# Pool waits by tile for the second phase of an attention, channel mix and expert kernel

## The chip, the cores and the metric

The kernel runs on one core of one Trainium2 chip. The metric is the device time of one execution in microseconds (us).

## The reference

Three parts follow each other on a batch of 4. The first is attention with 8 heads of 64 over 32 global and 512 local positions: the global queries see everything, the local ones the global keys and a band of 32 positions on either side. Its output (4 x 544 rows, 512 wide) goes through a channel mix: `r * v` with `v = relu(xk @ w_k)^2 @ w_v` and `r = sigmoid(xr @ w_r)`, where `xk` and `xr` blend each row with the one before it. The last part sends each of the 2176 rows to one of 8 experts:

```python
for s in range(S):
    fresh_e = int(np.argmax(logits[b, s]))
    if s == 0 or local_gate[b, s] < 0.5: e = fresh_e
    else: e = prev_e if prev_e >= 0 else fresh_e
    prev_e = e
    ls = logits[b, s] - logits[b, s].max()
    p = np.exp(ls)
    p /= p.sum() + 1e-09
    h = np.maximum(x[b, s] @ w1[e], 0.0)
    out[b, s] = p[e] * (h @ w2[e])
```

`w1` is 512 x 1024 and `w2` 1024 x 512 for each expert. All is float32.

## The kernel before

Each float32 product is made of three matmuls on a high and a low half (`mm3`, lines 19 to 24): an operand is copied into a tile of rounded values by ScalarE (ACT), and the rest is taken by a subtraction on VectorE (DVE) or GpSimd (POOL).

**Phase 1** (`phase1`, line 702) computes attention, channel mix and routing. The order of its work is written by a planner (`Sched`) with costs and priorities. Its tiles in SBUF lie in the pools `cf` (the mask, two `xT`, the weights `wr`) and `cs` (all else), its tiles in PSUM in two more; all four are closed at the end of phase 1. Each row is stored to `y` in DRAM. Routing leaves lists of rows by expert: `idx` (row numbers, 128 per chunk), `pcol` (gate values) and `counts` (chunks per expert). Already in phase 1, expert 0's first chunk of 128 rows is computed in gaps of TensorE (`ahead`, line 788); its output `oa` lies in `cs` and goes to `out` by an indirect DMA on GpSimd's queue (line 844).

**Phase 2** (`Experts`, lines 845 to 972) runs the eight experts. Line 996 opens its pools over the bytes that phase 1 gave back: `xwork` (two staging tiles `sw`, the gathered rows `xs1`, three pairs of transposed rows `x`), `work` (`hh`, `hl`, `hs`, `osb`), the PSUM pools `pst` (transposes, tag `pt`) and `ps2` (`ph` and `po`), and line 998 `wq` (weight slot 3). The pool `right` is older: it holds `xs0`, the staging tiles `st` and slot 2, and is in use in phase 1 already. `run` stands under a manual schedule, so that each engine keeps the written order:

```python
for k in range(K): s.gather(0,k)
_,cs=s.nc.values_load_multi_w_load_instructions(s.counts[0:1,0:E],...); cmax=...
for hf in range(2): s.prep(at(0,0),0,hf)
s.gather(1,0)
s.fetch()
for e in range(E):
    s.first(at(e,0),at(e,1),e,cs[e],...)
```

`gather` (line 857) fetches 2 x 128 rows of `y` by two indirect DMAs on GpSimd's queue, into `xs0` for the even and `xs1` for the odd chunk pairs. Line 950 loads the counts into registers of every engine. `prep` (lines 858 to 867) transposes the rows on TensorE into `pt` (line 864), ACT copies them into `xh` (line 866), DVE subtracts into `xl` (line 867). `fetch` starts weight loads of 512 KB each on SyncE's queue (line 767) into whatever staging tile is free, `st` or `sw`; `whole` (lines 776 and 779) splits a staged part into high and low on ACT and on DVE or POOL, and fetches the next.

`first` (line 933) decides by the expert's count, on every engine, with the branches of lines 937 and 941: two or more chunks take `full` (two chunks at once, lines 868 to 884) and then `more` (branches of lines 930 and 931); a single chunk takes `tail` (lines 885 to 913). In both the splits of the next expert's weights (`W`) and the transposes of its first chunks (`X`) are mixed in at fixed places. Here expert 0 has one chunk left and takes `tail`: its hidden layer goes into `pht` (line 905), its output into `po` (line 918), with expert 1's transposes after the first and fourth of eight steps of the output. `output` scales `po` into `osb` on DVE and scatters it to `out` by an indirect DMA (line 923).

The order at the seam of the two phases comes from these: the program order of each queue, the waits that a closed pool leaves to the next one on its bytes, and the branch at line 937.

## Time and profile before

| what | value |
|---|---|
| median of 3 runs | 809.23 us (805.88 to 812.53) |
| the profiled execution | 809.45 us |
| its span, first to last instruction | 807.7 us |
| busy: PE | 743.1 us (92%) |
| busy: DVE | 521.9 us (65%) |
| busy: ACT | 398.6 us (49%) |
| busy: POOL | 370.8 us (46%) |

All times in the text are us from the start of the span. PE is TensorE, PEld its weight loads, which run beside its matmuls; DVE is VectorE, ACT ScalarE, POOL GpSimd, SP SyncE. A `q` behind an engine's name means its sequencer, which waits, branches and issues DMAs. "Idle before" is the time that an engine stood still ahead of an instruction, and the releaser is what ended it, as inferred from semaphores; the one put down is the last by the profile, which is not always the one that was binding.

### The profile page before, as it was taken

What the parts mean: (1) busy time and instruction counts of PE and PEld (TensorE: products, weight loads), DVE (VectorE), ACT (ScalarE), POOL (GpSimd) and SP (SyncE); (2) the same over time, 40 slices, a digit from 0 to 9 for tenths busy, and PEclk for the clock granted to TensorE, in tenths of its full rate; (3) what the DMA queues carried; (4) which work ended last, traced back from release to release, by engine and by line L of the source; (5) the groups of instructions that cost most, each with busy time, mean ns of one, the idle gap of its engine ahead of it and who ended that gap; (6) DMA issues with size and microseconds to landing.
All of it is one profiled execution on the core that took longest, in us unless ns stands there. A gap on an engine that the chain in (4) does not pass through costs nothing. (4 is left out here: it accounts for less than half of the span.)

```text
span 807.7 us, 14233 instructions
## 1 busy us (share of the span) xinstructions
PE 743.1 (92%) x4790; PEld 626.2 (78%) x4790; DVE 521.9 (65%) x1482; ACT 398.6 (49%) x985; POOL 370.8 (46%) x495
## 2 busy tenths in 40 slices
PE   5988799899989999899999999986899999999974
PEld 3655687698878888888887888865698999998953
DVE  6699789776695785785675855664772725435531
ACT  4787676663555654655553523414661615224420
POOL 6678968645254362654462333115753513324130
PEclk9998999999999999899999899998999999999987
DMA  6674341211102102112001400317874524517210
GB/s 151 160 190 141 84 114 56 76 23 47 41 19 76 35 18 67 40 33 63 22 2 61 149 27 14 131 40 258 286 266 148 189 103 131 177 61 253 87 53 7
DMA packets 93966, 78.71 MB, mean 97 GB/s; under 512 B 70559, under 2 KB 74655, under 8 KB 93859
## 3 DMA queue, kind: packets, MB, share of 16 engines
q1 hardware_dynamic: 89618, 64.27, 26.7%
q0 software_dynamic: 4240, 13.11, 4.8%
q8 instruction: 54, 0.88, 0.5%
q14 instruction: 54, 0.43, 0.2%
HBM read 68.44 MB, written 9.70 MB: 97 GB/s over the span
## 5 line engine op out<-in xcount | busy, mean ns | idle before, releaser
L222 POOL TENSOR_SCALAR pl<-pl,mx 128x192 f32<-128x192 f32 (+1 forms) x128 | 66.9, 535 | 75.7 <-DVE mx L219 42.8
L216 ACT ACTIVATE pl<-pl,mx 128x224 f32<-128x224 f32 (+1 forms) x128 | 58.8, 461 | 35.3 <-DVE mx L213 30.4
L21 PE MATMUL psk<-xs,slot0h 128*128 128x256 f32 x256 | 75.3, 299 | 0.9 <-ACT xs L448 0.8
L23 PE MATMUL psk<-xs,slot0h 128*128 128x256 f32 x256 | 74.0, 290 | 0.0
L24 PE MATMUL psk<-xs,slot0l 128*128 128x256 f32 x256 | 73.9, 290 | 0.0
L857 POOL DMA_INDIRECT xs<-y,idx x32 | 39.9, 1246 | 70.8 <-PE pt L864 42.1
L923 POOL DMA_INDIRECT out_dram<-osb,idx x19 | 23.5, 1238 | 95.4 <-DVE osb L922 79.9
L450 POOL TENSOR_TENSOR xs<-xm,xs 128x512 fp32r<-128x512 f32 (+1 forms) x36 | 46.2, 1293 | 44.3 <-ACT xs L448 44.3
L878 ACT ACTIVATE hh<-ph 128x256 fp32r<-128x256 f32 x56 | 21.6, 385 | 84.1 <-PE ph L24 82.9
L443 POOL TENSOR_SCALAR xm<-xT,mut 128x256 f32<-128x256 f32 (+7 forms) x96 | 42.9, 465 | 29.5 <-DVE xT L294 16.2
L21 PE MATMUL psv<-slot1h,kh 128*128 128x512 f32 x136 | 55.6, 410 | 0.0
L23 PE MATMUL psv<-slot1l,kh 128*128 128x512 f32 x136 | 54.8, 404 | 0.3 <-POOL slot1l L417 0.3
L24 PE MATMUL psv<-slot1h,kl 128*128 128x512 f32 x136 | 54.7, 405 | 0.0
L21 PEld LDWEIGHTS psk<-xs,slot0h 128*128 128x128 f32 x256 | 49.4, 195 | 2.3 <-ACT xs L448 1.2
L23 PEld LDWEIGHTS psk<-xs,slot0h 128*128 128x128 f32 x256 | 49.8, 195 | 0.7
L24 PEld LDWEIGHTS psk<-xs,slot0l 128*128 128x128 f32 x256 | 49.6, 194 | 0.5
L228 PE MATMUL ptp<-ident,pl 128*128 128x128 f32 x256 | 45.1, 298 | 4.7 <-DVE qT L119 1.4
L236 PE MATMUL av<-ph,v 128*128 128x256 f32 x192 | 44.6, 292 | 2.3 <-DVE xT L294 1.0
L119 DVE TENSOR_TENSOR plo<-ptp,ph 128x512 fp32r<-128x512 f32 x48 | 32.8, 685 | 19.4 <-ACT ph L117 19.1
L879 DVE SCALAR_TENSOR_TENSOR hl<-ph,hh 128x256 fp32r<-128x256 f32 x56 | 23.7, 423 | 33.0 <-ACT hh L878 32.6
L446 DVE SCALAR_TENSOR_TENSOR xm<-xT,mut,xm 128x256 f32<-128x256 f32 (+7 forms) x96 | 40.3, 456 | 3.6 <-POOL xm L443 3.5
L228 PEld LDWEIGHTS ptp<-ident,pl 128*128 128x128 f32 x256 | 32.1, 152 | 11.5 <-POOL pl L222 3.9
(730 smaller groups left out, 2491.9 us busy)
## 6 DMA issues: line engine op xcount, KB each, us to landing
st<-in_moe_w_dram SPq DMA_DIRECT2D x42, 512.0 KB, 4.6
sw<-in_moe_w_dram SPq DMA_DIRECT2D x22, 512.0 KB, 4.8
y<-r SPq DMA_DIRECT2D x17, 256.0 KB, 2.1
qn<-in_q_l_dram SPq DMA_DIRECT2D x32, 128.0 KB, 3.0
kn<-in_k_l_dram SPq DMA_DIRECT2D x32, 128.0 KB, 3.0
earlyh<-in_moe_w_k_dram SPq DMA_DIRECT2D x8, 512.0 KB, 5.0
raw<-in_moe_w_v_dram SPq DMA_DIRECT2D x8, 512.0 KB, 4.0
vn<-in_v_l_dram SPq DMA_DIRECT2D x24, 96.0 KB, 2.1
```

The costliest lines, as they stand in the source:

```text
L21: i=nc.tensor.matmul(out,wh,xh,start=first,stop=False)
L23: nc.tensor.matmul(out,wh,xl,start=False,stop=False)
L24: return nc.tensor.matmul(out,wl,xh,start=False,stop=last)
L119: nc.vector.tensor_sub(out[1],x,out[0].bitcast(F32))
L216: nc.scalar.activation(p[:,h,ks],p[:,h,ks],AF.Exp,bias=mx[:,h:h+1],scale=-1.0,accum_out=mx[:,4+h:5+h])
L222: nc.gpsimd.tensor_scalar(out=p[:,h,ks],in0=p[:,h,ks],scalar1=mx[:,6+h:7+h],scalar2=0.0,op0=ALU.mult,op1=ALU.add)
L228: nc.tensor.transpose(pt[:,c,h],p[:,h,c*96:c*96+P],s.ident)
L236: nc.tensor.matmul(o,s.v(u,x,i,c),P_[y][:,c],start=c==m==0,stop=c==1 and m==len(parts)-1)
L443: nc.gpsimd.tensor_scalar(out=x[:,u,o:o+k],in0=s.xT[b][:,c,q:q+k],scalar1=m[:,1,c:c+1],scalar2=0.0,op0=ALU.mult,op1=ALU.add)
L446: nc.vector.scalar_tensor_tensor(out=x[:,u,o:o+k],in0=s.xT[b][:,c,1+q:1+q+k],scalar=m[:,0,c:c+1],in1=x[:,u,o:o+k],op0=ALU.mult,op1=ALU.add)
L450: nc.gpsimd.tensor_sub(xl[:,cs,:n],x[:,:,:n],xh[:,cs,:n].bitcast(F32))
L857: s.nc.gpsimd.indirect_dma_start(out=s.xs[i][:,j,:],out_offset=None,in_=s.y,in_offset=IndirectOffsetOnAxis(ap=s.idx[:,ch:ch+1],axis=0))
```

## The change

The pools that phase 2 opens are declared with `reuse_waits="tile"` in place of the default `"pool"`. With the default, the first instruction on a pool that lies on bytes given back by another waits for the users of the whole pools that lay there. With `"tile"`, the first write of each tile waits for the users of the bytes under that tile. Sizes, places, instructions and their written order are as before.

```diff
--- before.py
+++ after.py
@@ -993,9 +993,10 @@
             m=phase1(tc,st,ins,const,y,ident,x,slots,early,place,right)
             x.idx,x.pcol,x.counts,x.cmax=m.idx,m.acc[:,E*NCH:],m.ci,m.cm
 
-        x.xwork=p("xwork"); x.work=p("work"); x.ps=Pools("pt",p("pst",space=PSUM),p("ps2",space=PSUM))
+        t=dict(reuse_waits="tile")
+        x.xwork=p("xwork",**t); x.work=p("work",**t); x.ps=Pools("pt",p("pst",space=PSUM,**t),p("ps2",space=PSUM,**t))
         x.alloc()
-        slots.append(pair(p("wq"),3))
+        slots.append(pair(p("wq",**t),3))
         with tc.manual_schedule():
             x.run()
```

## Rows read from the trace of the kernel before

**Rows 1.** PE's waits, 535 to 808: us in total, times, longest.

```profile
PE pt L864 <- DMA xs<-y,idx: 4.4, 3, 2.3
PE pht L21 <- ACT xh L866: 3.4, 1, 3.4
PE pht L21 <- DMA st<-in_moe_w_dram: 2.5, 1, 2.5
```

**Rows 2.** Stretches: length; busy PE, PEld, DVE, ACT, POOL; clock, DMA share, GB/s.

```profile
543.00:550.00 7.00, 2.09 (x14) 1.50 (x13) 1.24 (x3) 0.92 (x2) 1.34 (x2) 0.76 0.23 82
550.00:558.50 8.50, 8.49 (x31) 6.42 (x31) 5.19 (x6) 5.15 (x7) 6.88 (x5) 0.79 0.83 254
558.50:562.00 3.50, 0.56 (x3) 0.40 (x4) 1.23 (x1) 1.54 (x2) 2.69 (x3) 1.00 1.04 392
568.00:574.00 6.00, 3.54 (x10) 2.80 (x10) 5.52 (x5) 3.17 (x3) 5.09 (x3) 0.72 0.88 313
574.00:776.00 202.00, 201.26 (x1256) 180.33 (x1255) 104.25 (x134) 85.08 (x135) 75.78 (x50) 1.00 0.48 162
```

**Rows 3.** Timeline of the seam: start, length, instruction [idle before <- releaser].

```profile
540.30 0.97 POOL L857 DMA_INDIRECT xs<-y,idx  x1 [19.04 <-DVE cint L699]
...
541.58 0.94 POOL L857 DMA_INDIRECT xs<-y,idx  x1 [0.30 <-issue]
...
544.55 1.03 POOL L844 DMA_INDIRECT out_dram<-oa,idx  x1 [2.03 <-DVE acc L683]
...
545.41 0.98 PE L864 MATMUL pt<-ident,xs 128*128 128x128 f32 x7 [1.46 <-DMA xs<-y,idx]
549.09 1.09 ACT L866 ACTIVATE xh<-pt 128x512 fp32r<-128x512 f32 x2 [12.22 <-DMA out_dram<-oa,idx]
549.51 1.68 SPq L767 DMA_DIRECT2D sw<-in_moe_w_dram  x2
549.69 0.98 POOL L857 DMA_INDIRECT xs<-y,idx  x1 [4.11 <-ACT xh L866]
...
549.85 0.77 PE L21 MATMUL pht<-slot2h,xh 128*128 128x512 f32 x1 [3.45 <-ACT xh L866]
```

**Rows 4.** The chain of waits, 540 to 575: start, length, what.

```profile
544.55 4.35 DMA out_dram<-oa,idx
...
553.55 8.15 DMA xs<-y,idx
```

**Rows 5.** SyncE's own waits, 535 to 575.

```profile
SPq L767 <- DMA out_dram<-oa,idx: 5.1, 1, 5.1
```

**Rows 6.** Users of `xT` and `wrh`: durations min/median/max in ns, first and last start.

```profile
L446 DVE SCALAR_TENSOR_TENSOR xm<-xT,mut,xm x96: 239/470/1251, 75.4 to 495.4; 128x256 f32<-128x256 f32 x40, 128x32 f32<-128x32 f32 x8, 128x224 f32<-128x224 f32 x8, 128x64 f32<-128x64 f32 x8
...
L24 PE MATMUL psr<-wrh,xs x68: 387/393/504, 119.3 to 517.0; 128*128 128x512 f32 x68
```

**Rows 7.** Sequencers on line 937 (540 to 556) and line 21 (549 to 550).

```profile
L937 PEldq COMPARE_BRANCH  x1: 3693/3693/3693, 545.4 to 545.4; - x1
L937 ACTq COMPARE_BRANCH  x1: 50/50/50, 549.1 to 549.1; - x1
...
L21 PEldq EVENT_SEMAPHORE  x5: 51/51/51, 549.3 to 549.7; - x5
```

**Rows 8.** Timeline of the second half of expert 0.

```profile
553.55 1.97 POOL L857 DMA_INDIRECT xs<-y,idx  x1 [0.30 <-issue]
...
558.53 1.06 ACT L776 ACTIVATE slot3h<-sw 128x1024 fp32r<-128x1024 f32 x1 [1.49 <-DMA sw<-in_moe_w_dram]
...
560.74 0.30 PE L864 MATMUL pt<-ident,xs 128*128 128x128 f32 x1 [2.25 <-DMA xs<-y,idx]
...
561.74 0.55 PE L864 MATMUL pt<-ident,xs 128*128 128x128 f32 x3 [0.71 <-DMA xs<-y,idx]
```

**Rows 9.** Sequencers on line 937 (560 to 575), and the stretch of PE's branch.

```profile
L937 PEldq COMPARE_BRANCH  x1: 4653/4653/4653, 565.2 to 565.2; - x1
...
565.15:569.80 4.65, 2.86 (x13) 2.01 (x12) 4.17 (x5) 3.66 (x5) 4.06 (x3) 1.00 0.80 273
```

## The prediction

> **What bounds the kernel now.** I first asked what TensorE (PE) waits for between the end of phase 1 and the end of the kernel [rows 1]: only 4.4 us for gathered rows (DMA into `xs`), 3.4 us once put down to `xh` of line 866, and 2.5 us once put down to a weight load. Then the table by stretches [rows 2]: from 574 to 776 us PE is busy 201.26 of 202.00 us, so whatever is won or lost at the seam is carried to the end unchanged, and nothing that the other engines gain after 574 counts. What is to be had lies at the seam: 543 to 550 us (PE busy 2.09 of 7.00), 558.5 to 562 (0.56 of 3.50) and 568 to 574 (3.54 of 6.00).

> The timeline of the seam [rows 3] with the chain [rows 4] shows the pool waits at work. The output of expert 0's first chunk leaves by the scatter of line 844, issued at 544.55, landed 4.35 us later, at 548.90. It reads a tile of phase 1's pool `cs`. Three things start at once behind it: ACT's `xh` at 549.09, SyncE's two `sw` loads at 549.51, GpSimd's gather for `xs1` at 549.69. The wait list of SyncE gives 5.1 us to it by name [rows 5]. None of the three needs that scatter's data or bytes: by the shapes, `cf` fills about 34.7 KB per partition (mask 0.9, two `xT` of 8.7, two `wr` of 8.2), and `xwork` is put on the same start: `sw0`, `sw1`, `xs1`, `x0h` take its first 16 KB, over mask and `xT`, and `x0l` the next 4, over `xT` and `wr`. `xT` is last read by an instruction that starts at 495.4 us, `wr` by one at 517.0 us [rows 6].

> **The change, part by part.**

> *Part 1, the waits at the seam.* Removed: the wait of `xh`, of the `sw` loads and of the `xs1` gathers for line 844. Nothing is added to the work; each first write of a phase 2 tile gets waits of its own, on users that ended long before. The transposes of the first chunk end at 546.39 (545.41 plus 0.98) [rows 3], four of the eight some 0.4 us sooner, so `xh` can start at about 546.1, 3.0 us earlier. SyncE can issue the `sw` loads when its reading of the counts is through, at 543.8, where its wait begins by subtraction (548.9 less 5.1), so 5.7 us earlier. GpSimd issues gathers 1.28 us apart (540.30, 541.58): the two for `xs1` follow at about 542.9 and 544.1, line 844 at 545.4, and the two for expert 1 (which wait for the transposes to let go of `xs0`) at about 546.7 and 548.0, the second 5.5 us before its 553.55 of now [rows 3, 8].

> *Part 2, PE's start into expert 0.* It is tempting to book the 3.0 us of `xh` here, for the wait list does [rows 1]. But PE's sequencer reaches the branch of line 937 at 545.4, as soon as the second gather lets the transposes go, and takes 3693 ns over it, to 549.1; five waits at line 21 follow at an even pace until 549.8 [rows 7], and the matmul starts at 549.85. PE starts late by itself; `xh` only came out at the same moment. ACT takes 50 ns over the same branch [rows 7], so this is not the price of the decision as such. The branch hangs on the second gather (541.58, arrived 545.41), which does not move. So I book nothing here, and a loss: with 0.23 of the DMA engines' time taken (543 to 550 us [rows 2]) the branch lasted 3.69 us, at 565.15 with 0.80 taken it lasted 4.65 [rows 9]. Now 1 MB of weights will move while it runs. Bounds 0 and +0.96 us; I take +0.5, since the loads begin only with it.

> [...]

> *Part 3, the stall at 558.5.* In the second half of expert 0, PE waits for the first chunk of expert 1: 2.25 us and then 0.71 us [rows 8], 2.96 together. The second of its two gathers was issued at 553.55 and took 8.15 us to land [rows 4], since two `sw` loads, three `st` loads and four gathers shared 13 us; from 558.5 the DMA share is 1.04 [rows 2]. Issued at 548.0 and landing even as slowly as that, it is there at 556.2, 2.3 us before PE comes for it at 558.5; if GpSimd takes line 844 first, each gather is about 1.7 us later and lands at 557.9, still in time. So 2.96 us go, bounds 0 and 2.96. What is late next: ACT's `slot3h` from `sw`, which waited 1.49 us for its load [rows 8], now 5.7 us early; after 562 PE has no wait of that size before the branch at 565.15.

> *Part 4, the entry into expert 1.* PE idles 2.46 us before 574 (6.00 less 3.54 [rows 2]; the wait list has it as 2.5 behind a weight load [rows 1]); the branch of 4.65 us at 565.15 covers it, less what PE still had queued [rows 9]. A lighter DMA load could bring it to 3.69, so bounds 0 and -0.96; the traffic there is the same splits and gathers, shifted with PE, so I take 0. The clock: the granted clock averages 0.76 from 543 to 550, 0.79 from 550 to 558.5 and 0.72 from 568 to 574 [rows 2], each time beside an idle stretch of PE. A low stretch costs about 1.7 us (0.28 of 6.00; 0.21 of 8.50 is 1.8). Which of them falls where when work is shifted by 3 us I can't tell: -1.7 to +1.7, taken as 0.

> *Part 5, more and smaller waits.* The first touch of a tile in each arm of an `If` may carry waits of its own. PE's at line 21 come about 0.1 us apart (five from 549.3 to 549.7, each 51 ns long) [rows 7]. They show only where PE's sequencer is not ahead, at the slow branches; bounds -0.5 (all five go) and +0.5 (five more), taken as 0. PSUM: `pst` lies on phase 1's small pool and `ps2` on the big one, whose users are all done by 549.85; the transposes already ran at 545.41, so nothing comes of these pools.

> **The sum.** 807.7 us of span, +0.5, -2.96, gives 805.2; with the 1.75 us that the profiled execution has outside its span (809.45 less 807.7), 807.0. That execution lay 0.22 above the median of the runs (809.23), so 806.8 there, which is -0.3%. One per cent is 8.1 us, about what a measurement of this kernel can tell from no change; the three runs themselves lie 6.65 apart. This will look like no change.

> **The rivals.**

> *The seam opens at its first end too* (0.16). PE was waiting for `xh` after all, or the branch ends sooner. Then PE starts 0.76 us after `xh` as now (549.85 less 549.09), at 546.9, another 2.95 us gone and no loss on the branch: 809.23 - 2.96 - 2.95 = 803.3. For it: the wait list. Against it: the branch record, and the five waits behind it, none of which is longer than 51 ns [rows 7].

> *The early loads get in the way* (0.15, slower). The `sw` loads start at 543.8 beside the gather that the branch hangs on. If that gather takes 8.15 us as under load, not 3.83 (541.58 to 545.41), PE starts 4.32 us later; with the branch at 4.65, +5.28, less the 2.96: +2.3, or 811.6. It decides the sign as soon as gather and branch together lose more than 2.96 us. Against it: the gather has 2.3 us of its 3.83 behind it when the loads are issued, and PE starts into a clock that is then sooner back.

> [...]

> *The stall is only moved, or the waits stay* (0.19). The `xs1` gathers or the `sw` loads keep a late wait, because some user of the bytes is counted later than the shapes say, or the option does nothing where it stands; or the freed transfers end as late and PE waits elsewhere by 570. Time 809.2 (0 from the sum). For it: the DMA share of 1.04 at 558.5, so that the bytes may be the limit, not the issue. Against it: from 543 to 550 the share is 0.23 [rows 2], which leaves room for 2.1 MB (0.77 of 7.00 us at the 392 GB/s of 558.5 to 562).

> **How the numbers follow.** Forecast 806.8 with 0.50; the rivals 803.3 with 0.16, 811.6 with 0.15, 809.2 with 0.19. The range reaches to the second at its upper end, and to the first with most of the 1.7 us of the clock at its lower: 802.0 to 811.6. Faster by over 1% needs less than 801.1: the first rival and more than one clock loss gone, 0.04. Slower by over 1% needs 817.3: the second rival and 5.7 us more, 0.03. The rest, 0.93, is within 1%.

> **What would show it.** Right: `xh` at about 546, the `sw` loads at about 544, the gathers for expert 1 before 550, no wait for `xs` at 558, and PE's start into expert 0 still within 1 us of 549.85 behind a branch of 3.7 to 4.7 us. Wrong: PE starting before 548.5 (first rival), the second gather landing after 547 (second), or a wait of over 2 us between 555 and 568 (third).

## The result, and the profile after

The changed kernel takes 817.14 us in the median of 8 runs (811.79 to 820.51), the kernel before, run beside it, 808.95 (805.88 to 812.53). The ratio is 1.0115, 95% interval 1.0089 to 1.0141: slower, against a forecast of 0.3% faster. The profiled execution lasts 820.03 us, its span 818.2.

The same instructions run on every engine, apart from waits that are instructions of their own (`EVENT_SEMAPHORE`): of these PE runs 235 where it ran 256. The timeline of the seam, then of PE behind its entry into expert 1:

```profile
542.72 0.97 POOL L857 DMA_INDIRECT xs<-y,idx  x1 [19.04 <-DVE cint L699]
...
543.99 0.94 POOL L857 DMA_INDIRECT xs<-y,idx  x1 [0.30 <-issue]
...
546.25 0.97 SPq L767 DMA_DIRECT2D sw<-in_moe_w_dram  x2
...
546.97 1.03 POOL L844 DMA_INDIRECT out_dram<-oa,idx  x1 [2.03 <-DVE acc L683]
...
548.24 0.98 PE L864 MATMUL pt<-ident,xs 128*128 128x128 f32 x7 [1.87 <-DMA xs<-y,idx]
...
548.82 1.09 ACT L866 ACTIVATE xh<-pt 128x512 fp32r<-128x512 f32 x2 [9.55 <-PE pt L864]
...
552.10 0.94 POOL L857 DMA_INDIRECT xs<-y,idx  x1 [0.30 <-issue]
...
552.20 2.69 SPq L767 DMA_DIRECT2D st<-in_moe_w_dram  x3
...
555.03 0.77 PE L21 MATMUL pht<-slot2h,xh 128*128 128x512 f32 x1 [5.81 <-DVE slot1l L779]
...
575.59 0.77 PE L21 MATMUL pht<-slot1h,xh 128*128 128x512 f32 x1 [6.03 <-DVE slot2l L779]
581.67 0.79 PE L23 MATMUL pht<-slot1l,xh 128*128 128x512 f32 x1 [5.32 <-issue]
```

Here the end of phase 1 falls 2.4 us later than in [rows 3] (compare the first gather, 542.72 and 540.30), which is a difference between two executions. Counted from there, the change does what it says. `xh` follows the transposes within 0.6 us, the `sw` loads go out ahead of the scatter of line 844, the second gather for expert 1 starts 9.38 us behind the first of all instead of 13.25 [rows 3, 8], and the wait for expert 1's rows near 558 [rows 8] is gone. Yet PE starts expert 0 5.18 us later than before, 2.76 us later when it is counted from the first gather.

PE's waits from 535 us on:

```profile
PE pht L21 <- DVE slot2l L779: 6.0, 1, 6.0
PE pht L21 <- DVE slot1l L779: 5.8, 1, 5.8
PE pht L23 <- issue: 5.3, 1, 5.3
...
PE pt L864 <- DMA xs<-y,idx: 1.9, 1, 1.9
```

The first two are the entries into experts 1 and 0, which were 2.5 and 3.4 us [rows 1]. `slot1l` and `slot2l` are only the last things that happened to end before PE went on. The third, 5.3 us after a single matmul of expert 1, has no counterpart before; no semaphore ends it. The sequencers on line 937 and on line 21 tell more:

```profile
L937 PEldq COMPARE_BRANCH  x1: 6473/6473/6473, 548.3 to 548.3; - x1
...
L937 PEldq COMPARE_BRANCH  x1: 8535/8535/8535, 566.7 to 566.7; - x1
L937 ACTq COMPARE_BRANCH  x1: 55/55/55, 567.0 to 567.0; - x1
...
L21 PEldq EVENT_SEMAPHORE  x1: 51/51/51, 554.9 to 554.9; - x1
```

PE's branch lasts 6.47 and 8.54 us (3.69 and 4.65 before [rows 7, 9]), ACT's stays at 0.05. Ahead of the first matmul stands one semaphore wait instead of five [rows 7]. The stretches (length; busy PE, PEld, DVE, ACT, POOL; clock, DMA share, GB/s):

```profile
548.25:555.03 6.78, 0.97 (x8) 0.77 (x8) 4.84 (x5) 3.92 (x5) 3.82 (x4) 0.72 0.92 274
555.03:566.70 11.67, 11.67 (x53) 9.53 (x54) 3.83 (x5) 5.75 (x8) 5.06 (x3) 0.87 0.62 213
566.70:575.59 8.89, 2.86 (x14) 2.04 (x13) 8.33 (x6) 4.49 (x5) 7.33 (x5) 0.79 0.94 298
575.59:586.00 10.41, 5.09 (x12) 3.71 (x13) 1.23 (x1) 1.06 (x1) 0.00 (x0) 0.53 0.64 224
586.00:786.00 200.00, 199.94 (x1250) 179.53 (x1249) 103.58 (x133) 85.05 (x135) 75.50 (x50) 1.00 0.45 154
```

Nearly everything is decided before 586: behind it PE is busy 199.94 of 200 us, as in the last row of [rows 2], and its one longer idle time after that, at the entry into expert 7, is 4.74 us (5.20 before). In both entries the DMA share is over 0.9; from 543 to 550 it had been 0.23 [rows 2], in the second branch 0.80 [rows 9]. In the fourth row the granted clock is 0.53 (0.50 up to 585.43, 1.00 from there), but PE works only half of that stretch.

What moves while the branch lasts can be read from the view of the DMA queues (packets, MB, share of 16 engines). First the changed kernel from 548.25 to 552.30, the first 4 us of the branch; then 552.30 to 553.40; then, for the stop after 576.36, 575.3 to 579.3 and 579.3 to 580.5:

```profile
q1 hardware_dynamic: 364, 0.84, 64.9%
q0 software_dynamic: 143, 0.50, 36.3%
...
q8 instruction: 1, 0.02, 5.5%
...
q1 hardware_dynamic: 543, 1.09, 82.3%
q0 software_dynamic: 99, 0.30, 18.3%
...
q8 instruction: 1, 0.02, 4.9%
```

And the kernel before, from 545.43 (where its branch begins) to 546.90:

```profile
q0 software_dynamic: 71, 0.25, 44.6%
q8 instruction: 1, 0.02, 4.7%
```

The idle times of PE over 0.5 us from 538 us on add up to 16.1 us before and 23.8 now. The 7.7 us between them are +2.36 (into expert 0), -2.96 (rows for expert 1), +3.57 (into expert 1), +5.32 (the stop) and -0.6 elsewhere. The spans of the two executions differ by 10.5 us, of which 2.4 lie ahead of the first gather; the medians differ by 8.2.

### The profile page after: what moved, and what is told of

It reads as the page before. It is cut to its first block, busy times and chain, and to the rows that moved or that the text cites. A ratio compares the mean times of both kernels' runs of the same rounds, so it can differ in the third digit from the quotient of the medians.

```text
span 818.2 us, 14211 instructions
## 1 busy us (share of the span) xinstructions
PE 745.9 (91%) x4790; PEld 628.6 (77%) x4790; DVE 522.4 (64%) x1482; ACT 398.4 (49%) x985; POOL 370.2 (45%) x495
## 4 chain that ended last, share of the span: by engine, by line
PE 69%; DVE 12%; DMA 8%; issue 4%; POOL 3%; ACT 2%; SPq 1%; POOLq 0%; DVEq 0%; ACTq 0%
DMA xs<-y,idx 5%; PE av L236 4%; PE psk L21 4%; PE psk L23 4%; PE psk L24 4%; PE psv L21 4%; PE psv L24 4%; PE psv L23 3%; PE po L24 3%; PE po L21 3%; PE po L23 3%; PE ph L23 3%; PE ph L24 3%; PE ph L21 3%; PE ptp L228 3%
```

## The experiments

Theory A: the change sends loads and gathers out earlier, and they get ahead of PE's fetches of code. Theory B: the changed waits themselves cost. Theory C: it is the gathers, not the loads, that stand in the way.

**First four runs.** `sw_late` and `xs_late` were to put the `sw` loads, or the `xs1` gathers, back behind the scatter of line 844, all else by tile. `before_load` leaves the waits of before and adds two loads of 512 KB, from DRAM to DRAM, whose data nobody uses. `after_hint` is the changed kernel with two branch hints for PE: the one for expert 0's arm lands at the start of PE's program, the one for expert 1's at the start of expert 0's arm.

```diff
# sw_late (xs_late the same way, with xs1)
+        x.xsw=p("xsw"); x.xwork=p("xwork",**t); ...
-        new=[s.xwork.tile([P,1024],...
+        new=[s.xsw.tile([P,1024],...
# before_load
         s.gather(1,0)
+        for i in range(2): s.part(2,i,s.dm[i])
         s.fetch()
# after_hint
-        with tc.If(c>=2) as two:
+        with tc.If(c>=2,label=f"ex{e}") as two:
+        tc.mark_branch_hint_location("ex0","LikelyTaken",[mybir.EngineType.PE])
         for hf in range(2): s.prep(at(0,0),0,hf)
             if f==TW[2]: turn(1,hs[1])
+            if f==TW[2] and e==0 and k==0: s.tc.mark_branch_hint_location("ex1","LikelyTaken",[mybir.EngineType.PE])
```

> The two staging tiles of the early weight loads lie alone in a pool that keeps the waits by pool; all other phase 2 pools wait by tile. Theory A (PE's slow branch is a fetch of instructions that queues behind the data transfers which the change starts earlier, above all the two weight loads of 512 KB): the loads go out some 5 us later, behind the scatter, PE's first branch falls from 6.5 to between 3.7 and 4.7 us, and the time lies at or below that of the kernel before, 804 to 811 us. Theory B (the changed waits themselves hold PE, whatever moves): nothing comes back, 814 to 820 us and a first branch of 6 us or more. Theory C (it is the gathers that stand in the way, not the loads): the first branch stays over 5.5 us and the time over 812 us.

> The gathered rows xs1 lie alone in a pool that keeps the waits by pool, so that the gathers of expert 0's odd pair and those of expert 1 behind them go out some 4 us later; the weight loads stay early. Theory A (loads in front of PE's instruction fetch): the first branch stays at 5.5 us or more and the time at 813 to 820 us. Theory C (gathers in front of it): the first branch falls to 3.7 to 4.7 us and the time to 811 us or less. Theory B (waits as such): 814 to 820 us.

> The kernel before, with two extra transfers of 512 KB, from the weights in DRAM to a DRAM tile that nobody reads, issued on SyncE's queue where the changed kernel issues its two early weight loads; all waits are those of the kernel before. Theory A: PE's first branch rises from 3.7 to 5.5 us or more though no wait changed, and the time by 2 to 6 us, to 811 to 815 us. Theory B: branch 3.7 us and the time within 2 us of the kernel before, since the branch has nothing to do with transfers.

> The changed kernel with two branch prefetch hints for PE, one for the branch into expert 0 (it stands at the start of the program's first block) and one for the branch into expert 1 (at the start of expert 0's last arm). Theory A: if a hint has the target fetched ahead of the branch, the branch into expert 1 falls from 8.5 us to under 1 us and 4 to 8 us of the time go, to 809 to 813 us; the hint for expert 0 stands some 540 us ahead and may be without effect. Theory B: no branch changes and the time stays at 814 to 820 us.

`sw_late`: 816.37 us, ratio 1.0098 (1.0060 to 1.0137). `xs_late`: 820.19, 1.0121 (1.0069 to 1.0174). Both missed their aim: the new pools lie over the mask and `xT`, which were long done, so the loads still went out at 543.7 and the gathers at 547.5, ahead of the scatter. They are little more than two further samples of the changed kernel.

`before_load`: 811.80, 1.0026 (0.9998 to 1.0054). Its first branch and its wait:

```profile
L937 PEldq COMPARE_BRANCH  x1: 6657/6657/6657, 542.5 to 542.5; - x1
```
```profile
PE pht L21 <- ACT xh L866: 6.4, 1, 6.4
```

With no wait changed, two loads alone stretch the branch from 3.69 to 6.66 us. That settles the kind of cause for the first entry, against B. (The wait is put down to `xh`, which itself came only at 548.96, behind a scatter that landed as late; so the measure here is the branch, not the idle time.)

`after_hint`: 802.16, 0.9918 (0.9893 to 0.9943): 15 us less than the changed kernel, where 4 to 8 had been expected of A, and faster than the kernel before. Its branches last 0.40 and 1.71 us; PE's waits at the seam:

```profile
PE pt L864 <- DMA xs<-y,idx: 3.3, 3, 2.0
PE po L21 <- ACT hh L895: 1.3, 1, 1.3
```

**Runs five to eight.** `before_hint`: the kernel before with the same hints. `loads_late` and `gathers_late`: the two that missed their aim again, with the new pool behind `xwork`, where its bytes reach into `cs`. `xwork_pool`: one part of the change alone.

```diff
# loads_late (gathers_late the same way, with xs1)
+        x.xwork=p("xwork",**t); x.xsw=p("xsw"); ...
# xwork_pool
-        x.xwork=p("xwork",**t); ...
+        x.xwork=p("xwork"); ...
```

> The kernel before with the two prefetch hints for PE (expert 0's and expert 1's single-chunk arm), no wait changed. Theory A (the change lets data transfers go ahead of PE's late instruction fetches, and has a gain of its own beside it): both branches of line 937 fall under 2 us here too, but PE's start into expert 0 stays at about 549.9, since xh still waits for the scatter of line 844 until 549.1; the stall of 2.96 us for expert 1's rows at 558 stays; the 2.46 us at 570 go. So about 806.5, ratio 0.995 to 1.000, and 3 to 6 us over the 802.16 of the changed kernel with the same hints: with the fetch out of the way the change is a gain. Theory B (the changed waits themselves cost): the hints are worth the same 15 us on both kernels, so about 794, ratio 0.98. Theory C (the gathers in the way): no word on this one; within 1 us of the kernel before.

> The changed kernel, with the two staging tiles sw in a pool of their own with pool waits, placed behind the rest of xwork so that its bytes reach into those of phase 1's pool cs: the two loads of 512 KB wait for the scatter of line 844 again (at about 549.5 instead of 546), all else waits by tile. Theory A: PE's first branch is back at 3.5 to 4.5 us instead of 6.47, PE starts into expert 0 at about 549.5 or sooner; the later part less certain, since the next loads come as late as in the kernel before: second branch 4 to 7 us. About 807 to 813, ratio 0.998 to 1.005. Theory B: 817, as the changed kernel. Theory C (gathers, not loads): the first branch stays over 6 us, 815 to 818.

> The changed kernel, with xs1 alone in a pool of its own with pool waits, placed behind the rest of xwork and so reaching into the bytes of cs: the two gathers for xs1, and those for expert 1 behind them on GpSimd's queue, wait for the scatter of line 844 again, all else waits by tile, the loads of sw go out early. Theory A: PE's first branch stays at 5.5 to 7 us, since 1 MB of loads still goes ahead of its fetch; the stall of 2 to 3 us for expert 1's rows at 558 to 562 is back; 816 to 821, ratio 1.009 to 1.015. Theory C: the first branch is back at 4 us, 810 to 813. Theory B: 817.

> One part of the change: only work, wq and the two PSUM pools wait by tile, xwork (sw, xs1, the three pairs x) by pool as before. Theories A and C: nothing that moves a transfer is left of the change, so as the kernel before, ratio 0.997 to 1.003, first branch 3.5 to 4 us, the stall at 558 as before. Theory B (the waits themselves, of which PSUM's and those of work are part): between the two kernels or as the changed one, 812 to 817.

`before_hint`: 804.81, 0.9972 (0.9943 to 1.0001). The hints are worth 2 us here and 15 in the changed kernel, which goes against B. Its branches last 0.40 and 2.94 us, the second over the 2 us expected. Its waits:

```profile
PE pt L864 <- DMA xs<-y,idx: 4.3, 4, 1.8
PE pht L21 <- ACT xh L866: 1.5, 1, 1.5
PE pht L21 <- ACT slot2h L776: 0.8, 1, 0.8
```

With the branches that short, PE does wait for `xh` (1.5 us) and for expert 1's rows (2.3 of the 4.3 us), and the change takes 0.5% off (0.9918 against 0.9972: some 4 us, with intervals that just meet; 2.7 us by the medians).

`xwork_pool`: 807.69, 0.9996 (0.9962 to 1.0031), branches of 3.89 and 6.11 us. Without `xwork`'s tiles the rest of the change loses nothing that shows.

`loads_late`: 814.05, 1.0103 (1.0070 to 1.0136). `gathers_late`: 807.16, 1.0002 (0.9962 to 1.0042). Both came out opposite to A's numbers. Their branches, first those of `loads_late`, then of `gathers_late`:

```profile
L937 PEldq COMPARE_BRANCH  x1: 5353/5353/5353, 541.6 to 541.6; - x1
...
L937 PEldq COMPARE_BRANCH  x1: 8315/8315/8315, 559.5 to 559.5; - x1
```
```profile
L937 PEldq COMPARE_BRANCH  x1: 5903/5903/5903, 543.0 to 543.0; - x1
...
L937 PEldq COMPARE_BRANCH  x1: 5773/5773/5773, 562.3 to 562.3; - x1
```

At the first branch loads alone (5.90) and gathers alone (5.35) cost about as much as both (5.9 to 7.1 in seven kernels), so A and C are each half right there. The difference of 7 us lies behind it: `loads_late` has the stop of 5.28 us, `gathers_late` has none. That led to theory D: the second branch's length goes by how long before it the reloads of `sw` were issued, and a long branch pushes the next fetch behind the next loads.

**Runs nine to twelve.** Each hint alone; the reloads held back until after PE's branch; and a third hint, for expert 7.

```diff
# reload_held, in step(), after a split
+            i=8*p[0]+4*p[1]+p[2]
+            if i in (11,12): return
+            if i==13: s.free.insert(0,s.free.pop())
         s.fetch()
# hint_three: after_hint, and in full()
+            if j and e==E-2 and k==0: s.tc.mark_branch_hint_location(f"ex{E-1}","LikelyTaken",[mybir.EngineType.PE])
```

> The changed kernel with the hint for expert 0's arm alone. Theory D, what the runs so far have made of A: PE's branches wait for a fetch of code behind data; at the second entry the length goes by how long before PE's branch the reloads of sw were issued (6.5 us in the kernel before, 3.1 in the changed one), and a branch that lasts over 6 us pushes the fetch of the next code behind the next loads. So here: first branch under 1 us, 4 to 5 us of idle time gone there, but the distance at the second entry stays near 3 us, the branch there at 6 to 8.5 us, and the stop of 4 to 5 us behind it stays. About 812, ratio 1.002 to 1.007. Rival (the second entry only suffers from what the first one left behind): both entries mend, 802 to 805.

> The changed kernel with the hint for expert 1's arm alone. Theory D: first branch 6 to 6.5 us with 5 to 6 us idle as in the changed kernel; second under 2 us; no stop of 4 to 5 us behind it, since the next code is asked for ahead of the next loads. 4.7 and 5.3 us of idle time gone: about 807, ratio 0.995 to 1.001. Rival (the stop behind the second entry is a late fetch of its own, whatever the branch lasted): the stop stays, 811 to 813.

> The changed kernel without hints; the reloads of the two sw tiles in expert 0's arm are held back and go out behind the next reload of st, that is some 1 to 2 us behind the start of PE's branch into expert 1 instead of 3 us ahead of it. Theory D: that branch 3.5 to 5 us, idle 1 to 3 us there, no stop of 5 us behind it, first branch as in the changed kernel; 806 to 810, ratio 0.996 to 1.003, if no split waits longer for the later loads. Theory C (the gathers are what the fetch waits for): no gather moves, the branch stays over 6 us, 814 to 818. Theory B: 817.

> The changed kernel with three hints: expert 0's and expert 1's arm as before, and expert 7's, at the start of expert 6's two-chunk arm. The branch into expert 7 (3.86 us at 770 with two hints, 4.60 us of idle time behind it) should fall under 1 us and the idle time to 0 to 1.5 us: 798 to 800, ratio 0.985 to 0.990. If a hint that lies that far ahead of its branch (with line 931's branch between) does nothing: 802, ratio 0.992.

`hint_first`: 808.28, 0.9993 (0.9972 to 1.0014). The first entry mends; at the second the branch lasts 6.13 us and PE idles 7.17, in one piece: it loads the weights of its first matmul and only then stops, so no separate stop follows. `hint_second`: 811.42, 1.0025 (1.0002 to 1.0048); neither long branch nor stop at expert 1, 5.52 us left at expert 0, and a new wait of 2.6 us behind it for `hs`, which ACT writes at line 907. Either is 4 us off D's number, on opposite sides.

`reload_held`: 813.81, 1.0053 (1.0021 to 1.0084). The second branch falls from 8.54 to 5.32 us with no gather moved, as D has it; but the stop stays, which D excluded:

```profile
L940 PEldq COMPARE_BRANCH  x1: 5315/5315/5315, 567.9 to 567.9; - x1
```
```profile
PE pht L23 <- issue: 5.1, 1, 5.1
```

`hint_three`: 800.08, 0.9862 (0.9829 to 0.9894). The branch into expert 7 falls from 3.86 to 1.78 us and the idle time there from 4.60 to 2.55 (under 1 us and at most 1.5 had been expected). This is the fastest version of the study.

**The last four.** Theory E: the stop is a matter of where the code lies. In all of its first five appearances PE stops at the same instruction, right behind the first matmul; with one instruction more ahead (the hint of `hint_first`) it stops one instruction sooner. The change takes semaphore waits out of PE's program, and some of these are instructions. Ahead of the first matmul of expert 0's arm the trace has five before [rows 7] and one after (above), at line 864 up to the entry into expert 1 two and one, and ahead of the first matmul of expert 1's arm, before and after:

```profile
L21 PEldq EVENT_SEMAPHORE  x4: 51/51/51, 570.0 to 570.4; - x4
```
```profile
L21 PEldq EVENT_SEMAPHORE  x1: 51/51/51, 575.5 to 575.5; - x1
```

Arms that are not taken leave nothing in a trace. If the two-chunk arms of experts 0 and 1 lost as many as the single-chunk arms beside them, four and three, then 1 + 4 + 4 + 3 = 12 instructions fewer stand ahead of expert 1's arm. The shift kernels move that arm's place by repeated transposes in arms that are never taken: `after_shift` and `held_shift` (`reload_held` moved) by 12, to where it lay before, and `hint_shift` is `hint_three` moved by 12. `before_shift` moves it by 240, which is 16 back if code lies in blocks of 256 instructions (an estimate: from the q8 packet at 30.64 us to the one at 528.65, 26 packets on, PE runs 6634 instructions in the kernel before, 255 for each; the third arm, not taken either, fills each shift up to 256, so that later code keeps its place): there its first matmul, with four waits ahead of it and not one, stands within an instruction of where the change puts it.

```diff
# after_shift (before_shift: 120 and 8)
-                nc.tensor.transpose(pt[:,d,...
+                for _ in range(1+s.rep): nc.tensor.transpose(pt[:,d,...
+                s.rep=0
+            s.rep=6 if e==1 else 0
             s.full(i,e,0,list(W),[*own,*X])
-                again()
+                again(); s.rep=122 if e==1 else 0
```

> The changed kernel with 12 PE instructions (6 repeated transposes) put into expert 1's two-chunk arm and 244 into its empty arm, neither of which is taken: expert 1's single-chunk arm lies 12 instructions later, as in the kernel before, everything else as before modulo 256 instructions. Theory E (place of the code): the stop of 5 us behind the first matmul of expert 1 is gone, first branch 6 to 6.5 us and second 6 to 8.5 us as in the changed kernel; about 811 to 813, ratio 1.002 to 1.006. Rival (the stop comes of loads ahead of the next fetch, wherever the code lies): the stop stays, 816 to 818, ratio 1.009 to 1.012.

> The kernel before with 240 PE instructions in expert 1's two-chunk arm and 16 in its empty arm, neither taken: expert 1's single-chunk arm lies where it lies in the changed kernel (within an instruction), no wait changed. Theory E: a stop of 2 to 5 us appears right behind the first matmul of expert 1; 811 to 814, ratio 1.003 to 1.006. Rival: no stop, as the kernel before, ratio 0.997 to 1.003.

> reload_held with the 12 instructions of after_shift: the reloads of sw go out behind PE's branch and expert 1's arm lies as in the kernel before. Theory E with D: second branch 4 to 5.5 us, idle 1.5 to 3 us there, no stop behind it, first branch still 6 us: 807 to 810, ratio 0.997 to 1.002, so that what is left of the loss is the first branch alone, which the gone stall for rows pays for. Rival: as reload_held, 812 to 815.

> hint_three with the 12 instructions of after_shift. If the place of the arm still matters with the target asked for ahead (the block behind it is late as well): 797 to 799, ratio 0.981 to 0.985, the idle times of 1.3 and 2.1 us at 566 and 570 smaller. If the hint covers it: as hint_three, 800, ratio 0.985 to 0.988.

`after_shift`: 811.85, 1.0019 (0.9991 to 1.0047). PE's waits:

```profile
PE pht L21 <- DVE slot1l L779: 5.3, 1, 5.3
PE pht L21 <- issue: 4.1, 1, 4.1
PE pt L864 <- DMA xs<-y,idx: 1.7, 1, 1.7
```

The stop is gone, and with it most of the loss, with no wait, load or gather changed. `before_shift`: 812.78, 1.0045 (1.0015 to 1.0075). PE's timeline behind its entry into expert 1:

```profile
567.83 0.77 PE L21 MATMUL pht<-slot1h,xh 128*128 128x512 f32 x1 [4.21 <-DMA st<-in_moe_w_dram]
568.39 0.63 PE L23 MATMUL pht<-slot1l,xh 128*128 128x512 f32 x1
572.09 0.80 PE L24 MATMUL pht<-slot1h,xl 128*128 128x512 f32 x1 [3.07 <-issue]
```

The kernel before, moved, has the stop, behind its second matmul. Both go for E. Like the branches, the stops of all six kernels that have one, and the idle time of `hint_first` at expert 1, end 2.3 to 2.6 us behind the start of a q8 packet. `held_shift`: 809.89, 1.0013 (0.9987 to 1.0039), second branch 4.95 us, no stop. `hint_shift`: 801.34, 0.9887 (0.9839 to 0.9934), no different from `hint_three`: with the hints given, the place no longer shows.

PE's idle times at the seam (over 0.5 us, read from PE's waits and timeline of each) beside the ratios. Left out are the wait for expert 0's rows ahead of the branch, 1.45 to 2.07 us in all of them, and a few short ones further on, the longest 1.43 us in `held_shift`:

| kernel | into expert 0 | rows for expert 1 | into expert 1 | stop | sum | ratio |
|---|---|---|---|---|---|---|
| before | 3.45 | 2.96 | 2.46 | - | 8.87 | 1 |
| `xwork_pool` | 3.72 | - | 3.88 | - | 7.60 | 0.9996 |
| `gathers_late` | 5.24 | 0.55 | 3.23 | - | 9.02 | 1.0002 |
| `held_shift` | 5.87 | - | 2.41 | - | 8.28 | 1.0013 |
| `after_shift` | 5.31 | - | 4.07 | - | 9.38 | 1.0019 |
| `before_load` | 6.41 | 2.38 | 1.62 | - | 10.41 | 1.0026 |
| `before_shift` | 3.88 | - | 4.21 | 3.07 | 11.16 | 1.0045 |
| `reload_held` | 4.88 | - | 2.79 | 5.14 | 12.81 | 1.0053 |
| `sw_late` | 5.37 | - | 4.02 | 4.29 | 13.68 | 1.0098 |
| `xs_late` | 6.38 | - | 4.80 | 4.84 | 16.02 | 1.0121 |
| `loads_late` | 4.68 | - | 5.77 | 5.28 | 15.73 | 1.0103 |
| after | 5.81 | - | 6.03 | 5.32 | 17.16 | 1.0115 |

8.29 us lie between the sums of after and before, 8.2 between their medians. Counted from the kernel before, the ratios ask for 0 to 3.1 us more than the sums, which are those of one execution each; so the seam carries most of the loss. Two things stand out. The stall for expert 1's rows is no fixed cost of the kernel before: `xwork_pool` and `before_shift`, whose `xwork` waits as before, have none in their profiled execution. And where it is missing, the entry into expert 1 costs more: 2.96 + 2.46, 2.38 + 1.62, 0 + 3.88 and 0 + 4.21 add up to 5.42, 4.00, 3.88 and 4.21.

A likely reason can be read from SyncE's issues. From the first reload of `sw` to PE's branch 7.3 us go by in `before_load`, 6.5 before, 4.3 in `gathers_late`, 3.5 in `xwork_pool` and `before_shift`, 3.1 in `after_shift`, `sw_late`, `xs_late`, `loads_late` and after; the branch lasts 3.79, 4.65, 5.77, 6.11 and 6.43, then 6.6 to 8.5. A PE that is held up by rows comes to its branch later after these issues: before, 2.6 MB were moved from the first reload to the branch (398 GB/s over 6.51 us), in the changed kernel 0.6 MB (186 GB/s over 3.10 us). The reloads need not be through, though: before, they landed 9.4 and 8.7 us after 558.64 and 560.87, behind the start of the branch at 565.15. `reload_held` moved them behind the branch and cut it to 5.32 us, so they do bear on it; what else does stays open.

## Why the prediction was wrong

*Part 1, the waits at the seam*: right. `xh`, the loads and the gathers moved as worked out.

*Part 2, PE's start into expert 0*: right that the branch and not `xh` holds PE, so that the first rival fell (with the branch at 0.40 us, in `before_hint`, `xh` still holds PE for 1.5 us); wrong in the size. "Bounds 0 and +0.96 us; I take +0.5": the branch grew by 2.78 us and the idle time by 2.36. The upper bound was the branch of 4.65 us under a DMA share of 0.80 [rows 9]. But that share was a mean over the stretch, and in that branch q8's packets started 0.4 and 1.5 us after its begin; a row of a branch that begins with 1 MB already issued was not there. `before_load` measures it at +2.96.

*Part 3, the stall at 558.5*: the stall went, but its 2.96 us were no gain. What comes late next is the second branch, not the `slot3h` that I named: "after 562 PE has no wait of that size before the branch" looked for a wait, while PE, coming sooner, stood 8.54 us at the branch with a DMA share of 0.94, where it had been 4.65 us with 0.80.

*Part 4, the entry into expert 1*: the term of the sum that failed most. "the traffic there is the same splits and gathers, shifted with PE, so I take 0" (bounds 0 and -0.96). It is not shifted with PE: the reload is set by ACT's and DVE's splits, and the distance to PE's branch shrank from 6.5 to 3.1 us. It measured +3.57.

*Part 5, more and smaller waits*: asked only for the time of the waits. That they are instructions, that taking 12 away moves the code behind them, and that its place can bring a stop (3.07 us in `before_shift`) or take one away (5.32 us, `after_shift`), I didn't think of. The stop of 5.32 us is the largest single term of the loss, and no rival held it. So against the +0.5 and -2.96 of the sum stand +2.36, -2.96, +3.57 and +5.32. The clock, taken as 0, leaves no term that can be seen: the idle times (7.7 us) and the later end of phase 1 (2.4) make up 10.1 of the 10.5 us between the spans.

*The rivals.* "The early loads get in the way" was right that they do, but put the price on the gather (4.2 us, where I feared 8.15) and on 0.96 us of branch. Against the 3.83 us of before, the gather's 4.2 show little of the loads; what came late was the packet on q8 (4.1 us behind the start of the branch, 1.2 before). "The stall is only moved" was right for Part 3 alone. With the arm in its old place the change costs 0.2%, which its interval does not tell from nothing (`after_shift`, 1.0019); on the forecast's 809.23 that is 810.8 us, inside the range.

What stays open: why a packet on q8 starts late. That data stand ahead of it is inferred from when they were issued; the trace shows the packet, not the request. Nor does the trace show what the first hint sets off: in `after_hint` q8 has no packet between 528.0 and 549.8, and the branch at 545.46 lasts 0.40 us all the same. That a packet holds 256 instructions, which the shift kernels assume so as to leave all later arms in place, rests on the 255 to a packet counted above (254 in the changed kernel, over 25 packets from 31.02 to 506.81 us); the runs agree in so far as the idle time at expert 7's entry is 4.62 us in `after_shift` and 4.74 in the changed kernel.

## What to carry to other kernels

Where an engine's sequencer takes microseconds over a branch that costs others 0.05, ask what data will be in the queues when it gets there: with the loads freed from their wait PE's first branch lasted 6.47 us instead of 3.69, and two added loads alone made it 6.66 (`before_load`). A wait that is an instruction of its own (here PE ran 256 before and 235 after) moves all code behind it when it is removed, so before a change of waits is judged at a per cent, look whether a stop without a releaser sits near a branch, and try the same kernel with the arm moved by a few untaken instructions. Here the lasting remedy was to give PE hints ahead of its branches: with them the change is a gain of 2.7 us by the medians and some 4 by the ratios, and with three hints the kernel takes 800.08 us.

## What was unexpected of the hardware

The branch of line 937 into the arms of experts 0 and 1 cost PE 3.7 to 8.5 us where no hint was given, more with loads under way (3.69 before, 6.66 with the two loads of `before_load`), and 0.40 us at the first entry where a hint stood at the start of PE's program, some 545 us before the branch.

Right behind the first matmul of expert 1's arm PE stopped a second time, for 4.3 to 5.3 us, behind branches of 5.3 to 8.5 us; in `before_shift` it stopped behind the second matmul, for 3.07. I take it for the border of a fetch of code, since it goes by the place of the arm (`after_shift` has none); no view shows the border itself.

Moving one arm by 12 instructions that never run changed the time by 5 us (817.14 to 811.85; by the ratios, 1.0115 to 1.0019, nearly 8).
